# Score units of two banks that may take a third, P V sums in the last PSUM bank, a ring of exponentials, and two GELUs by tanh

## The chip, the cores and the metric

The kernel runs on one core of a Trainium2 chip. The metric is the device time of one execution in microseconds (us). Five engines work at the same time, each through its own queue in order: TensorE (PE, matrix products; PEld is its weight load), ScalarE (ACT, functions such as exp), VectorE (DVE, elementwise work and reductions), GpSimd (POOL), and SyncE (SP), which here only issues transfers. PSUM, where TensorE writes its results, has eight banks of 128 partitions x 512 float32 values; this text calls them b0 to b7.

## The reference

There are two layers, each an attention block and a mixer with an MLP, on 2048 tokens of 448 features with 16 heads of 28:

```python
x = x + _A_ref(_layernorm(x), A_wqkv, A_wo)
x = x + _B_ref(_layernorm(x), B_w1, B_w2, B_w3, B_w4)
x = x + _A_ref(_layernorm(x), A_wqkv, A_wo)
x = x + _B_ref(_layernorm(x), B_w1, B_w2, B_w3, B_w4)

def _A_ref(x, wqkv, wo):              # attention, 16 heads
    q, k, v = split(x @ wqkv)
    p = softmax(q @ k.T * Dh ** -0.5)
    return (p @ v) @ wo

def _B_ref(x, w1, w2, w3, w4):        # mixer, then MLP
    h = gelu(layernorm(x) @ w1)       # gelu in its tanh form
    g0, g1, g2, g3 = the four quarters of h's features, shifted by -1, +1, -2, +2 tokens
    x1 = x + concat(g0, g1, g2, g3) @ w2
    return x1 + gelu(layernorm(x1) @ w3) @ w4
```

## The kernel before

**The stream of score blocks.** A block is one head's scores for 512 (query, key) columns on 128 partitions: one PSUM bank. Both layers together have 2048 blocks, and their order is fixed: `segs` lists segments (a chunk of queries, a group of four heads, a range of key tiles) and `stream` their blocks. `t_scores` cuts the stream into units. An even unit has three blocks, in b0, b1, b2; an odd unit has two, in b3, b4 (`unit_banks`). One exponential of ScalarE (`t_exp`, L1892) reads a whole unit from PSUM and writes it, in bf16, to slots of the buffer `PT`, which has 15 slots. A unit's slots are fixed by its number: three pairs of units, five slots each. So unit u may write when P V has read unit u - 6. The scores of unit u + 2 go into the banks of unit u, and TensorE may start them when the exponential of unit u has ended.

**Blocks that VectorE takes.** Some blocks aren't given to ScalarE. `t_scores` takes a block further ahead in the stream and lets VectorE work out its exponential in five instructions (`d_first`, `d_chain`: L1736, L1763, L1765, L1767, L1770). Its scores stand either in the third bank of an even unit (rates `R_RATE`) or in a free shared bank (rates `D_RATE`). The tables of rates give, by stretch of the stream, the greatest share taken in this way.

**P V.** `t_pv` multiplies the exponentials by the values, eight blocks at a time, and sums a segment in one bank, b5, which it holds for the whole run. `t_norm` copies the sums out with VectorE (L1973, L1975).

**Shared banks.** All else that TensorE does goes through the list `MISC`: the projections of queries, keys and values, the output projection, the mixer's and the MLP's products (`mm4`, L1059: four column groups of 32 at a time). While the exponentials run, `misc` may take one of the first three names of the list. One of these is b5, which is never free, so there are two such banks, b6 and b7.

**The mixer and its GELU.** `t_mixA` works out the mixer's first product for a chunk of tokens. VectorE copies it out of PSUM (L2128), and its GELU is then done in one of two ways. Where `PAIR` names the chunk, one ScalarE instruction does all four feature groups (L2140), right after the GELU of an MLP group of tokens that `PAIR` names, so that both use one load of the function table (`ACT_TABLE_LOAD`). Otherwise `tanh_gelu` makes it from a tanh, which has the exponentials' table: a square (L2156, on GpSimd or VectorE), a VectorE instruction (L2157), the tanh (L2158), a VectorE instruction (L2159), for each feature group. `t_mixB` and `t_w4` go on with the MLP.

**Order.** `Sched` is a list scheduler that runs when the kernel is built: it has a cost for each operation, and ranks (`RANK`), rates, leads and first positions that say what goes first. Its result is an order of instructions on each engine's queue. Two further steps change that order: `P.rearranged(MOVES, WEAVE)` moves single operations, 370 of them, each named by its number, to written-out places, and `FILL_MORE` repeats six groups of filler matmuls. A filler (`filler`, L2385) is a product of the identity with itself into a bank that nobody uses, put in where TensorE has nothing to do in the plan (`keep_pe_busy`).

The last exponential is followed by the tail: `t_exp` sends the event `tail`, and the remaining MLP work then has all banks and plain GELUs on ScalarE (L2313, L2123).

Of the kernel before, what the change touches and what calls it, by code (L numbers as in the profile page):

```python
# [18 lines left out]
MOVES = (  # L19
# [147 lines left out]
    "stttsttttsttttstttsttsttsttsttttttttttvtttvttvtsttvstttvvtgttgvtvttgtgtvtvtgtvttsvtgtttdtttgttttttgttttvtttvtt",  # L167
    "tttttvtttttvtdtvttvttttttttttsttttsttttsttttsttttsttttsttttsttttsttttsttttsttttsttttsttttsttttsttttttttttttttv",
    "ttttdttttttttttvttttdttttttttttvttttdvttttdttttttttttvttttdttttttttttvttdvdd",
)  # L170

FILL_MORE = (
    (2714, 4), (2725, 9), (3749, 15), (5548, 4), (5564, 4), (9810, 14),
# [603 lines left out]
RHI = 7  # L777
# [1719 lines left out]
```

## Time and profile before

| what | value |
|---|---|
| median of 3 runs | 1024.59 us (1024.34 to 1025.14) |
| span of the profiled execution | 1022.4 us; its time outside the span isn't listed |
| ScalarE busy | 981.4 us (96%) |
| TensorE busy | 973.8 us (95%), of it fillers 150.1 us |
| VectorE busy | 811.0 us (79%) |
| first exponential starts, last one ends | 15.2 us, 968.4 us |
| exponentials | 782 instructions: 375 of three banks, 406 of two, one of one |
| blocks that VectorE takes | 109 |

A table of groups gives for each kind of instruction its count, the sum and the mean of the durations, and the engine's idle time ahead of it with what ended it. ScalarE starts its next instruction before the one ahead has left the pipeline, so the durations of neighbours overlap and their sum exceeds the busy time. The profile's times count from the first instruction.

### The profile page before, as it was taken

The page shows a single profiled execution, that of the slowest core. Times are in us where ns is not written, and L with a number is a line of the kernel's source. Part 1 is how long each engine was busy: PE and PEld are TensorE (multiplying, and loading weights), DVE is VectorE, ACT ScalarE, POOL GpSimd, SP SyncE. Part 2 cuts the span into 40 slices and gives each one's busy share as a digit, 9 for nine tenths or more (in the row PEclk, how much of TensorE's full clock was granted, in tenths as well). Part 3 has the DMA queues.
Part 4 walks back from the last instruction along what each step waited for, and adds up shares of the span by engine and source line. Part 5 has one row for each costly group of instructions (what it writes and reads, how often), then busy time and mean ns, then how long its engine had stood idle before and what let it go on. Part 6 is the DMA issues. An engine that isn't in the chain of part 4 may idle for free.

```text
span 1022.4 us, 36170 instructions
## 1 busy us (share of the span) xinstructions
PE 973.8 (95%) x16283; PEld 412.9 (40%) x16285; DVE 811.0 (79%) x1572; ACT 981.4 (96%) x894; POOL 292.3 (29%) x462
## 2 busy tenths in 40 slices
PE   8999999999999999999999999999999999999998
PEld 4332443443433254333433443433433433454565
DVE  8777999989888958876877868688898589866651
ACT  8999999999999999999999999999999999999942
POOL 3312021531453016252325112012624120532230
PEclk9999999999999999999999999999999999999999
DMA  4643413320321013131131024423302020121101
GB/s 126 161 111 117 119 45 79 53 39 23 76 61 28 13 37 96 23 48 34 48 111 38 33 69 134 141 66 99 65 25 37 17 68 16 31 57 31 26 12 33
DMA packets 99394, 62.57 MB, mean 61 GB/s; under 512 B 68712, under 2 KB 88552, under 8 KB 99240
## 3 DMA queue, kind: packets, MB, share of 16 engines
q1 hardware_dynamic: 99240, 60.27, 23.6%
q8 instruction: 127, 2.08, 0.9%
q14 instruction: 27, 0.22, 0.1%
HBM read 28.16 MB, written 16.76 MB: 44 GB/s over the span
## 4 chain that ended last, share of the span: by engine, by line
ACT 71%; PE 23%; DVE 4%; DMA 1%; issue 1%; DVEq 0%
ACT PT L1892 65%; PE ps L1059 14%; PE ps L1654 5%; PE ps L1050 4%; ACT h2T L2339 2%; ACT fb L2158 1%; PE ps L2385 1%; ACT L1892 1%; DVE PD L1770 0%; ACT hT L2140 0%; DVE h2T L2317 0%; DMA xT<-xn 0%; ACT L2339 0%; DMA obf<-in_A_x_dram 0%; DVE yd L1736 0%
## 5 line engine op out<-in xcount | busy, mean ns | idle before, releaser
L1892 ACT ACTIVATE PT<-ps 128x1024 bf16<-128x1024 f32 (+1 forms) x782 | 887.3, 1333 | 2.9 <-PE ps L1654 2.1
L1654 PE MATMUL ps<-qT,kT 32*128 32x512 bf16 (+1 forms) x2304 | 269.8, 335 | 24.2 <-ACT PT L1892 18.4
L1050 PE MATMUL ps<-PT,vaug 128*32 128x512 bf16 (+1 forms) x2420 | 246.1, 341 | 0.7 <-ACT PT L1892 0.2
L1059 PE MATMUL ps<-xT,w 128*32 128x512 bf16 (+4 forms) x2656 | 177.9, 344 | 4.2 <-DVE h2T L2317 2.2
L1654 PEld LDWEIGHTS ps<-qT,kT 32*128 32x128 bf16 x2304 | 69.7, 91 | 256.0 <-ACT PT L1892 227.0
L2385 PE MATMUL ps<-ident 128*32 128x256 bf16 x3524 | 150.1, 276 | 1.8 <-POOL ident L1144 1.5
L2385 PEld LDWEIGHTS ps<-ident 128*32 128x32 bf16 x3524 | 98.9, 97 | 28.5 <-issue 11.9
L1050 PEld LDWEIGHTS ps<-PT,vaug 128*32 128x32 bf16 x2420 | 74.0, 95 | 89.4 <-issue 71.0
L1999 POOL TENSOR_TENSOR otn<-ub,fb 128x512 bf16<-128x512 f32 (+1 forms) x31 | 34.7, 1120 | 210.3 <-DMA fb<-rscr 202.9
L1736 DVE TENSOR_SCALAR yd<-ps 128x512 int32<-128x512 f32 x109 | 74.6, 685 | 22.8 <-PE ps L1654 21.7
L1059 PEld LDWEIGHTS ps<-xT,w 128*32 128x32 bf16 (+1 forms) x2656 | 69.2, 95 | 56.7 <-issue 25.0
L1763 DVE SCALAR_TENSOR_TENSOR fb<-yd 128x512 f32<-128x512 uint16 x109 | 78.5, 724 | 0.8
L1765 DVE SCALAR_TENSOR_TENSOR fb<-fb,yd 128x512 f32<-128x512 f32 x109 | 77.9, 717 | 0.7
L1770 DVE SCALAR_TENSOR_TENSOR PD<-yd,PD 128x512 int16<-128x512 int16 x109 | 75.9, 698 | 1.6
L1059 PE MATMUL ps<-w,h2T 128*32 128x448 bf16 x1120 | 75.4, 355 | 1.1 <-ACT h2T L2339 1.0
L2317 DVE CAST h2T<-ps 128x512 bf16<-128x512 f32 (+1 forms) x70 | 44.4, 635 | 16.2 <-PE ps L1059 15.0
L1392 POOL TENSOR_TENSOR sq<-qT 128x512 bf16<-128x512 bf16 x24 | 28.5, 1190 | 96.2 <-DVE qT L1451 93.4
L1392 POOL TENSOR_TENSOR sq<-kT 128x512 bf16<-128x512 bf16 (+2 forms) x32 | 30.4, 950 | 83.0 <-DVE kT L1406 79.9
L1767 DVE TENSOR_SCALAR PD<-fb 128x512 bf16<-128x512 f32 x109 | 49.6, 456 | 1.0
L1059 PE MATMUL ps<-xT,wk_pad 128*32 128x512 bf16 (+2 forms) x576 | 47.6, 359 | 0.7 <-DVE kT L1406 0.3
L1654 PE MATMUL ps<-wk_pad,kT 32*128 32x512 bf16 x256 | 39.6, 384 | 4.6 <-ACT PT L1892 4.0
L1059 PE MATMUL ps<-xT,wq_pad 128*32 128x512 bf16 x512 | 43.2, 382 | 0.5 <-issue 0.5
(189 smaller groups left out, 1195.9 us busy)
## 6 DMA issues: line engine op xcount, KB each, us to landing
uscr<-ub SPq DMA_DIRECT2D x28, 256.0 KB
ub<-uscr SPq DMA_DIRECT2D x28, 256.0 KB, 6.8
fb<-rscr SPq DMA_DIRECT2D x24, 256.0 KB
xnd<-xn SPq DMA_DIRECT2D x28, 128.0 KB, 2.3
xd<-x_res SPq DMA_DIRECT2D x16, 224.0 KB, 2.1
x_res<-xd SPq DMA_DIRECT2D x16, 224.0 KB, 4.2
w<-in_B_w_dram SPq DMA_DIRECT2D x5, 448.0 KB, 6.0
obf<-in_A_x_dram SPq DMA_DIRECT2D x16, 112.0 KB
```

Of the source, the lines that this page charges most:

```text
L1050: return lambda e: e.matmul(out=out, lhsT=lhsT, rhs=rhs, start=start, stop=stop, **kw)
L1059: r.append(e.matmul(out=out[c:c + w, :], lhsT=lhsT[:, c:c + w], rhs=rhs, start=start, stop=stop, tile_position=(0, c)))
L1392: return both("sq", 0.15 + NW * 0.0018, 0.07 + NW * 0.00104, lambda e: e.tensor_tensor(out=sq[:, si, 0:NW], in0=src, in1=src, op=ALU.mult) ...
L1654: yield op("pe", (0.005 + NW * 0.00042) / nc_, lambda e, i=i, kc=kc, j=j, g=g, qt=qt, a=a, NW=NW, bank=bank: e.matmul(out=ps[:, bank, i * ...
L1736: yield op("dve", c_ps(512), lambda e: e.tensor_scalar(out=y, in0=ps[:, bi(bank), :], scalar1=SCALE * L2E * FS, scalar2=-126.0 * FS, op0=A ...
L1763: yield op(D_[0][0], D_[0][1], lambda e: e.scalar_tensor_tensor(out=q, in0=lo, scalar=E2 / E3 * FS, in1=lo, op0=ALU.add, op1=ALU.mult), re ...
L1765: yield op(D_[1][0], D_[1][1], lambda e: e.scalar_tensor_tensor(out=q, in0=q, scalar=E1 / E3 * FS * FS, in1=lo, op0=ALU.add, op1=ALU.mult) ...
L1767: yield op(D_[2][0], D_[2][1], lambda e: e.tensor_scalar(out=pdt, in0=q, scalar1=E3 / FS ** 3, scalar2=E0, op0=ALU.mult, op1=ALU.add), rea ...
L1770: yield op(D_[3][0], D_[3][1], lambda e: e.scalar_tensor_tensor(out=pdt.bitcast(I16), in0=hi, scalar=128.0, in1=pdt.bitcast(I16), op0=ALU. ...
L1892: yield op("act", 0.069 + n * w * 0.000833, lambda e, bk=bk, s0=s0, n=n, w=w: e.activation(out=PT[:, s0:s0 + n, 0:w], in_=ps[:, bk[0]:bk[0 ...
L2317: ev = op("dve", c_ps(m * NW), lambda e, hr=hr, pv=pv: e.tensor_copy(out=hr, in_=pv), reads=[("ps", bi(b))], writes=hk, touch=[b])
L2385: return [e.matmul(out=ps[32 * c:32 * c + 32, bi(b), 0:256].rearrange("p (a n) -> p a n", n=128), lhsT=ident[:, 32 * c:32 * c + 32], rhs=i ...
```

## The change

- `unit_banks`: an odd unit may have three banks: b3, b4 and b5. Before it forms an odd unit, `t_scores` adds a credit from the table `BX` (1 per odd unit where the table has no entry). With a full credit it asks for b5. It doesn't ask if b6 is in use or if an operation waits for a list that has b5 in it (`BXF`). If b5 is given, the unit takes three blocks, and the exponential gives b5 back.
- P V sums in b7 instead of b5, and holds it. The shared banks while exponentials run are therefore b6 and b5.
- A unit's slots in `PT` are no longer fixed: units follow each other in a ring of 15 slots, which starts again at slot 0 where a unit doesn't fit before the end. The exponential waits for P V of the blocks that had these slots last.
- `PAIR` loses (1, 4) and (1, 8): the GELUs of the mixer for tokens' tiles 4 to 7 and 8 to 11 of layer two are done by tanh.
- `MOVES`, `WEAVE` and `FILL_MORE` are empty: the order is the scheduler's own, and no filler group is repeated.
- The scheduler's numbers (`RANK`, `R_RATE`, `D_RATE`, `Q_LEAD`, first positions of K, Q and V, of weights, doubts and the windows for fillers) are others. The shares of `R_RATE`, weighted by blocks, sum to 187 blocks instead of 227, those of `D_RATE` to 276 instead of 284; `BX` asks on average for 0.80 of the odd units.

```diff
-MOVES = (
...
-WEAVE = (
...
-FILL_MORE = (
-    (2714, 4), (2725, 9), (3749, 15), (5548, 4), (5564, 4), (9810, 14),
-)
+MOVES = ()
+WEAVE = ()
+
+FILL_MORE = ()
...
-RHI = 7
+RHI = 9
...
-DTH = 0.4
-XSHUT = (8, 83)
+DTH = 0.396
+XSHUT = (12, 79)
...
-DDTH = 1.3
+DDTH = 1.876
...
-Sched.TARGET = 0.695
+Sched.TARGET = 0.684
...
+BX = {47: 0.25, 39: 0.75, 36: 0.25, 41: 0.5, 34: 0, 32: 0, 5: 1, 2: 0, 25: 0, 20: 0.75, 42: 0, 33: 1, 50: 0.25, 59: 0.25, 58: 0.75, 22: 0, 12: 0, 31: 1, 9: 1, 4: 1}
+BXD = 1.0
+BXF = 1
...
-PAIR = {(0, 12): 7, (1, 4): 0, (1, 8): 3}
+PAIR = {(0, 12): 7}
...
-        MISC = ["b6", "b7", "b5", "b4", "b3", "b2", "b1", "b0"]
+        MISC = ["b6", "b5", "b7", "b4", "b3", "b2", "b1", "b0"]
...
-            return (0, 1, 2)[:len(units[u])] if u % 2 == 0 else (3, 4)[:len(units[u])]
+            return (0, 1, 2)[:len(units[u])] if u % 2 == 0 else (3, 4, 5)[:len(units[u])]
...
                 lim = 3 - u % 2
+                if u % 2 == 1 and pos < len(stream):
+                    wide_t[0] += BX.get(seg_b0[stream[pos][0]] // 32, BXD)
+                    if wide_t[0] >= 1.0:
+                        got = None
+                        if not (BXF and (SC.busy.get("b6", False) or any(t_[3][0] == "acq" and "b5" in t_[3][1] for t_ in SC.pendq))):
+                            got = yield ("try", [["b5"]])
+                        if got is not None:
+                            lim = 3
+                            extra_bank.add(u)
+                            wide_t[0] -= 1.0
+                        wide_t[0] = min(wide_t[0], 1.0)
+                base = ring_at[0] if ring_at[0] + lim <= 15 else 0
                 while pos < len(stream) and len(un) < lim:
-                    if len(un) == 2 and rb is None and SC.load("dve", DWIN) < DTH:
+                    if len(un) == 2 and rb is None and u % 2 == 0 and SC.load("dve", DWIN) < DTH:
...
-                    home[blk] = ("pt", 5 * ((u // 2) % 3) + 3 * (u % 2) + len(un))
+                    home[blk] = ("pt", base + len(un))
...
                 units.append(un)
+                ring_at[0] = base + len(un)
+                before[u] = [owner[s_] for s_ in range(base, base + len(un)) if s_ in owner]
+                for k_, b_ in enumerate(un):
+                    owner[base + k_] = b_[0:2]
...
-                if u >= 6:
-                    for (si, kb, j) in units[u - 6]:
-                        yield ("wait", ("pv", si, kb))
+                for (si, kb) in before[u]:
+                    yield ("wait", ("pv", si, kb))
...
+                if u in extra_bank:
+                    yield ("rel", "b5")
...
-            yield ("acq", ["b5"])
+            yield ("acq", ["b7"])
...
-                                yield op("pe", max(0.018, 0.0015 + NW * 0.0001042), mm(ps[32 * j:32 * j + 32, 5, 0:NW], vaug[:, vs, 32 * (4 * g + j):32 * (4 * g + j) + 32],
+                                yield op("pe", max(0.018, 0.0015 + NW * 0.0001042), mm(ps[32 * j:32 * j + 32, 7, 0:NW], vaug[:, vs, 32 * (4 * g + j):32 * (4 * g + j) + 32],
...
-        SC.fill = (0.12, filler, ["b6", "b7", "b0", "b1", "b2", "b3", "b4"], lambda b: ("ps", bi(b)), [("ident",)])
+        SC.fill = (0.12, filler, ["b6", "b5", "b0", "b1", "b2", "b3", "b4"], lambda b: ("ps", bi(b)), [("ident",)])
```

More of the change, by code (lines that the diff above doesn't have):

```diff
@@ L802 @@
 SMALL = [11, 12]
-W_POS = (6, 9, 17, 5, 5, 5, 25, 21)
-V_FIRST = 1.366
-K_FIRST = (0.756, 0.932, 1.363)
-Q_FIRST = (0.531, 1.956, 2.405)
+BX = {47: 0.25, 39: 0.75, 36: 0.25, 41: 0.5, 34: 0, 32: 0, 5: 1, 2: 0, 25: 0, 20: 0.75, 42: 0, 33: 1, 50: 0.25, 59: 0.25, 58: 0.75, 22: 0, 12: 0, 31: 1, 9: 1, 4: 1}
+BXD = 1.0
+BXF = 1
+W_POS = (5, 7, 17, 8, 3, 7, 28, 23)
+V_FIRST = 1.113
+K_FIRST = (0.484, 0.789, 1.051)
+Q_FIRST = (0.3, 1.564, 2.358)
 Q_EARLY = 1
@@ L814 @@
 COLD = 6.0
-Sched.DOUBT2 = {"dma": 1.5, "pool": 0.2, "dve": 0.5, "act": 0.5, "pe": 0.0}
+Sched.DOUBT2 = {'dma': 1.5, 'pool': 0.2, 'dve': 0.5, 'act': 0.5, 'pe': 0}
 Sched.EARLY = 0.1
-Sched.DOUBT = {"dma": 0.8, "pool": 0.6, "dve": 0.05, "act": 0.05}
+Sched.DOUBT = {'dma': 0.8, 'pool': 0.6, 'dve': 0.05, 'act': 0.05}
+Sched.LCRED = 0.3
 def PENORM(L, ch, g):
@@ L903, in build_kernel @@
     units = []
+    extra_bank = set()
+    owner = {}
+    before = {}
+    ring_at = [0]
+    wide_t = [0.0]
     home = {}
@@ L1851, in t_scores @@
                 units.append(un)
+                ring_at[0] = base + len(un)
+                before[u] = [owner[s_] for s_ in range(base, base + len(un)) if s_ in owner]
+                for k_, b_ in enumerate(un):
+                    owner[base + k_] = b_[0:2]
+                if u in extra_bank and len(un) < 3:
+                    extra_bank.discard(u)
+                    yield ("rel", "b5")
                 blks, banks = list(un), [b_ for b_ in unit_banks(u)]
@@ L1892, in t_exp @@
                 yield op("act", 0.069 + n * w * 0.000833, lambda e, bk=bk, s0=s0, n=n, w=w: e.activation(out=PT[:, s0:s0 + n, 0:w], in_=ps[:, bk[0]:bk[0] + n, 0:w], func=ACT.Exp, scale=SCALE),
-                         reads=[("ps", b) for b in bk], writes=[("pt", s0 + k) for k in range(n)], tab="exp")
+                         reads=[("ps", b) for b in bk], writes=[("pt", s0 + k) for k in range(n)], tab="exp", touch=["b5"] if u in extra_bank else [])
                 for b in bk:
                     yield ("dead", "b%d" % b)
+                if u in extra_bank:
+                    yield ("rel", "b5")
                 yield ("sig", ("ex", u))
@@ L1920, in t_pv @@
                             yield ("wait", ("v", L, kt))
-                    yield ("ready", [home[(si, kb, j)] for kb in batch for j in range(4)] + ([("psw", 5)] if done == 0 else []))
+                    yield ("ready", [home[(si, kb, j)] for kb in batch for j in range(4)] + ([("psw", 7)] if done == 0 else []))
                     for kb in batch:
@@ L1972, in t_norm @@
             if first:
-                yield op("dve", c_ps(NW), lambda e: e.tensor_copy(out=u, in_=ps[:, 5, 0:NW]), reads=[("ps", 5)], writes=[uk])
+                yield op("dve", c_ps(NW), lambda e: e.tensor_copy(out=u, in_=ps[:, 7, 0:NW]), reads=[("ps", 7)], writes=[uk])
             else:
-                yield op("dve", c_ps2(NW), lambda e: e.scalar_tensor_tensor(out=u, in0=u, scalar=fct[:, L, PI[L, p], g:g + 1], in1=ps[:, 5, 0:NW],
+                yield op("dve", c_ps2(NW), lambda e: e.scalar_tensor_tensor(out=u, in0=u, scalar=fct[:, L, PI[L, p], g:g + 1], in1=ps[:, 7, 0:NW],
                                                                             op0=ALU.mult, op1=ALU.add),
-                         reads=[("ps", 5), uk, ("fct", L, PI[L, p])], writes=[uk])
+                         reads=[("ps", 7), uk, ("fct", L, PI[L, p])], writes=[uk])
             yield ("sig", ("ucopied", si))
```

124 lines of the change are left out of this document (10 added, 114 removed), and 46 rows, old and new, of the table MOVES.

## The prediction

> **What bounds the kernel now.** I read the page's head and its chain of waits first, then ScalarE's groups, its waits, and the stretches in which the bound changes.
>
> ```profile
> span 1022.4 us, 36170 instructions
> PE 973.8 (95%) x16283; PEld 412.9 (40%) x16285; DVE 811.0 (79%) x1572; ACT 981.4 (96%) x894; POOL 292.3 (29%) x462
> ACT 71%; PE 23%; DVE 4%; DMA 1%; issue 1%; DVEq 0%
> ```
>
> The chain that ended last is 71% ScalarE and 23% TensorE. Stretches (columns: TensorE, weight loads, VectorE, ScalarE, GpSimd busy, granted clock, DMA) say where each rules:
>
> ```profile
> 15.20:968.40 953.20, 910.02 (x14875) 373.30 (x14879) 780.12 (x1482) 949.30 (x846) 278.82 (x424) 1.00 0.25 61
> 892.60:903.20 10.60, 9.99 (x312) 7.85 (x306) 4.99 (x12) 10.56 (x5) 0.73 (x1) 1.00 0.05 16
> 903.20:968.40 65.20, 64.27 (x1160) 29.84 (x1156) 47.81 (x99) 65.18 (x63) 18.86 (x33) 1.00 0.17 42
> 968.40:1019.40 51.00, 51.00 (x1178) 32.42 (x1168) 18.63 (x38) 20.12 (x33) 8.19 (x20) 1.00 0.06 19
> ...
> 892.60:903.20 10.60, 6.86 (x244) 6.17 (x236) 1.00 0.05 16
> 903.20:968.40 65.20, 0.00 (x0) 0.00 (x0) 1.00 0.17 42
> ```
>
> The last two rows are of the fillers (L2385) alone. From the first exponential to the last (953.2 us) ScalarE idles 953.20 - 949.30 = 3.9 us: this phase is ScalarE's sum. The tail, 1022.4 - 968.4 = 54 us, is TensorE's: busy for all of 51 us. TensorE is full from 903.2 on, with no filler; just before, from 892.6 to 903.2, fillers take 6.86 us of it. So work that TensorE could do before 903 comes off the tail.
>
> **1. Fewer exponentials.** What does an instruction cost beside its data?
>
> ```profile
> L1892 ACT ACTIVATE PT<-ps 128x1536 bf16<-128x1536 f32 x375 | 582.8, 1554 | 2.2 <-PE ps L1654 1.5
> L1892 ACT ACTIVATE PT<-ps 128x1024 bf16<-128x1024 f32 x406 | 453.4, 1130 | 0.7 <-PE ps L1654 0.6
> ...
> L1892 ACT ACTIVATE PT<-ps 128x512 bf16<-128x512 f32 x1 | 0.6, 598 | 0.0
> L1892 ACT ACTIVATE PT<-ps 128x1536 bf16<-128x1536 f32 x39 | 62.8, 1611 | 0.0
> L1892 ACT ACTIVATE PT<-ps 128x1024 bf16<-128x1024 f32 x40 | 47.6, 1190 | 0.0
> 111.45 89.31 ACT L1892 ACTIVATE PT<-ps 128x1024 bf16<-128x1024 f32 x79
> ```
>
> The first three rows are the whole run. A bank more costs 1554 - 1130 = 424 ns. That would leave 1130 - 848 = 282 ns for an instruction, but neighbours overlap. The last three rows are one unbroken stretch: 79 instructions, 39 x 3 + 40 x 2 = 197 banks, in 89.31 us. 197 x 0.424 = 83.5, so an instruction costs (89.31 - 83.5) / 79 = 0.073 us, not 0.28.
>
> ScalarE's blocks: 375 x 3 + 406 x 2 + 1 = 1938. 782 are 391 pairs of units with 1938 / 391 = 4.96 blocks, 2.96 in the even unit and 2 in the odd. If no odd unit gets b5, 782 stay: 0 us. If all do, 1938 / 5.96 x 2 = 650: 132 fewer, 132 x 0.073 = -9.6 us. How often is b5 free? It is one of two shared banks now, and it is asked for only while b6 is free too:
>
> ```profile
> 511.00:562.00 51.00, 33.49 (x478) 12.23 (x471) 1.00 0.27 74
> L2317 DVE CAST h2T<-ps 128x512 bf16<-128x512 f32 x42 | 28.9, 689 | 10.0 <-PE ps L1059 9.1
> ```
>
> The stretch is of L1059 alone. A busy one keeps a bank for 33.5 us of products, and about 478 / 16 = 30 evacuations at 0.69 = 20.6 us: 54 of 102 bank-us, without the waits between. Both banks are then free for (1 - 0.53)^2 = 0.22 of the time at most; in quieter stretches more often. With a credit for 0.80 of the odd units I take 0.35: 1938 / 5.31 x 2 = 730 units, 52 fewer, **-3.8 us**.
>
> **2. TensorE's side of a unit.**
>
> ```profile
> 301.31 0.10 PEld L1654 LDWEIGHTS ps<-qT,kT 32*128 32x128 bf16 x3 [0.37 <-ACT PT L1892]
> 301.31 0.39 PE L1654 MATMUL ps<-qT,kT 32*128 32x512 bf16 x3
> ...
> 302.34 0.39 PE L1654 MATMUL ps<-qT,kT 32*128 32x512 bf16 x2
> PEld ps L1654 <- ACT PT L1892: 258.8, 668, 2.0
> ```
>
> Two or three blocks take the same 0.39 us, and ahead of them TensorE stands 0.37 us for a bank (258.8 us over 668 waits). A unit less frees up to 0.76 us of TensorE. Before 903 that becomes filler: 0. From 903 to 968 ScalarE runs 63 instructions; at most 9 units fewer would give 6.8 us, at 0.35 some 4, 3 us. But ScalarE is full there as well, so the end of the exponentials doesn't move by it, only the backlog of the tail. I count this under 4.
>
> **3. Two GELUs by tanh, on ScalarE and VectorE.**
>
> ```profile
> L2140 ACT ACTIVATE hT<-hT 112x2048 bf16<-112x2048 bf16 x2 | 3.8, 1906 | 0.0
> L2158 ACT ACTIVATE fb<-fb 112x512 f32<-112x512 f32 x16 | 12.2, 788 | 0.7 <-DVE fb L2157 0.7
> 414.86 1.04 ACT fb L2158 x2
> L2157 DVE SCALAR_TENSOR_TENSOR fb<-fb,hT 112x512 f32<-112x512 f32 x16 | 14.0, 882 | 0.6 <-POOL fb L2156 0.6
> L2159 DVE SCALAR_TENSOR_TENSOR hT<-fb,hT 112x512 bf16<-112x512 f32 x16 | 11.2, 702 | 2.4 <-ACT fb L2158 2.3
> ```
>
> Two GELUs of 1.906 = 3.8 us go, eight tanhs come: by the chain's pair 0.52 each, 4.2; at 0.788 alone, 6.3. So +0.4 (to +2.5); I take **+0.4**, the row where they stand in a full queue. The table loads stay: both GELUs used the load of an MLP group, which remains.
>
> ```profile
> L1763 DVE SCALAR_TENSOR_TENSOR fb<-yd 128x512 f32<-128x512 uint16 x109 | 78.5, 724 | 0.8
> L1765 DVE SCALAR_TENSOR_TENSOR fb<-fb,yd 128x512 f32<-128x512 f32 x109 | 77.9, 717 | 0.7
> L1770 DVE SCALAR_TENSOR_TENSOR PD<-yd,PD 128x512 int16<-128x512 int16 x109 | 75.9, 698 | 1.6
> L1736 DVE TENSOR_SCALAR yd<-ps 128x512 int32<-128x512 f32 x109 | 74.6, 685 | 22.8 <-PE ps L1654 21.7
> L1767 DVE TENSOR_SCALAR PD<-fb 128x512 bf16<-128x512 f32 x109 | 49.6, 456 | 1.0
> ```
>
> VectorE gets 8 x (0.882 + 0.702) = 12.7 us and perhaps squares, out of 953.2 - 780.1 = 173 us of idle time: 0. If they displaced blocks instead: a block costs VectorE the five rows, 3.28 us, and saves ScalarE 0.424, so four blocks go back, +1.7. The new rates and gates could move the 109 blocks by some 8 either way, 3.4 us. I take 0: the sums of the tables fall, while VectorE's gate (`DDTH`) opens.
>
> **4. The tail.**
>
> ```profile
> 891.82 0.68 DVE L2128 TENSOR_SCALAR hT<-ps 112x512 bf16<-112x512 f32 x1
> 892.59 1.28 ACT L2339 ACT_TABLE_LOAD   x1
> 893.09 6.62 PE L2385 MATMUL ps<-ident 128*32 128x256 bf16 x236
> 893.89 6.18 ACT L2339 ACTIVATE h2T<-h2T 128x7168 bf16<-128x7168 bf16 x1
> 899.97 1.90 ACT L2140 ACTIVATE hT<-hT 112x2048 bf16<-112x2048 bf16 x1
> 902.01 0.94 PE L1059 MATMUL ps<-w,hT 112*32 112x448 bf16 x16 [0.20 <-ACT hT L2140]
> ```
>
> This is the mixer's GELU for tiles 8 to 11, which becomes tanh. Its input is ready at 892.5, its output at 901.9; meanwhile TensorE makes 6.62 us of fillers, and the next real product waits for that output. With tanhs ahead of the table load the products could fill that hole. At most 6.9 us leave a stretch that is TensorE's to the end, with point 2 at most 10.7. Nothing leaves if the scheduler puts the tanhs after the table load, or if the last tokens' own chain sets the end. I take **-5**.
>
> **5. The order.** `MOVES` and `FILL_MORE` go. No row shows ScalarE under the plain order. Lower end 0: the shorter queue may need no repair. Upper end: from the end of an exponential TensorE needs 0.37 + 0.39 us and a hand-over, of the 0.92 us that a two-bank exponential lasts (2 x 0.424 + 0.073). Had one unit in ten (73) one product of four column groups in the way (0.2 us), that were 15 us. The nearest row is today's 3.9 us of idle time; I take as much again, **+4**.
>
> At no cost: the bank of P V (the same instructions); the ring (ScalarE's waits list none for P V, and 15 slots stay, two of which a lap may skip; up to +2); `misc`'s list in the tail. No DMA is added.
>
> **Sum.** -3.8 + 0.4 - 5 + 4 = -4.4. The profiled execution spans 1022.4, and 2.2 us lie between that and the median, 1024.6, if it ran like the three timed ones. 1022.4 - 4.4 + 2.2 = **1020.2 us**, faster by 0.43%. A measurement of this kernel tells some 0.2% (2 us) from no change.
>
> **Rivals.**
> - *The plain order loses more than the units give.* For it: the written-out order holds ScalarE's idle time at 3.9 us in 953, and the margin above is 0.1 to 0.2 us for each unit. Against: a three-bank odd unit leaves 0.42 us more margin. It decides from 8.4 + 2 = 10.5 us on; at 15 the time is 1024.6 - 8.4 + 15 = 1031. Slower.
> - *The shared bank starves the projections.* With b5 lent for about 2 us in a third of the odd units (137 x 2 = 274 bank-us of 1906), products come late, and the tail gets longer by a group's backlog. One MLP group of 14 products is about 14 x (0.23 + 0.69) = 13 us of one bank: 1020.2 + 9 = 1029 where two thirds of it stay on the path.
> - *It rarely does what it says.* b5 free for one odd unit in ten: -1 instead of -3.8, and -3 in the tail: 1025.
> - *All of it at once.* All odd units wide (-9.6), the whole hole filled (-6.9), the order free: 1024.6 - 9.6 - 6.9 + 0.4 = 1008.5.
> - *The clock falls.* The granted clock is 1.00 in every stretch above, the fillers' hole included. With fewer fillers, a stretch as long as that hole at half clock would cost its length, some 7 us, where TensorE is the bound: 1027.
>
> The Trainium skill, "TensorE: Matmul & The Clock Gate", Part 1: The HAM clock gate, says that an array idle for more than about 3.4 us falls to half its clock until it has been busy for a window. By that rule the six repeated filler groups matter only where TensorE would stand longer than that; the trace agrees as far as it goes, with a clock of 1.00 throughout, and can't show the fall.
>
> **Chances.** My forecast 0.34 (1016 to 1022.5), with the larger gain 0.14; the order 0.27, starved projections 0.12, the clock 0.04; rarely done 0.09. Faster 0.48, same 0.09, slower 0.43. About 0.1 lies below 1010 and 0.1 above 1032, where the order and the projections come together. The forecast's own range is 1015 to 1023.
>
> **What will show it.** Right: some 730 exponentials, over 400 of them of 1536 columns; ScalarE's idle time between exponentials under 9 us; 24 tanhs of 112x512; no fillers in the last GELU visit and a tail under 50 us. Wrong: ScalarE's waits for L1654 over 15 us (order), the tail over 58 us (projections), a granted clock under 1.00, or under 100 blocks on VectorE.

## The result, and the profile after

| | before | changed |
|---|---|---|
| time, median | 1024.46 us | 1035.68 us (1035.05 to 1038.23) |
| profiled execution: span | 1022.4 us | 1036.5 us |
| first exponential starts | 15.2 us | 16.0 us |
| first to last exponential: length | 953.1 us | 966.3 us |
| ... ScalarE busy in it | 949.3 us | 952.5 us |
| ... ScalarE idle in it | 3.9 us | 13.8 us |
| tail behind the last exponential | 54.1 us | 54.2 us |
| exponentials (blocks in them) | 782 (1938) | 771 (1943) |

The change makes the kernel slower: ratio 1.0115 [1.0101, 1.0130]. The forecast was 1020.2 us (1015 to 1023), with some 0.1 of the chances below 1010 and 0.1 above 1032. The 14.1 us between the two spans are 0.8 ahead of the first exponential, 3.3 of work on ScalarE, 9.9 of idle time between exponentials and 0.1 in the tail. The profiled execution of the changed kernel is the slowest of its four (1038.2 us, the others 1035.1 to 1036.3), so these parts add up to more than the 11.2 us between the medians.

The head of the changed kernel's page and its chain of waits:

```profile
span 1036.5 us, 34822 instructions
PE 961.9 (93%) x15627; PEld 402.5 (39%) x15629; DVE 822.9 (79%) x1575; ACT 984.6 (95%) x888; POOL 295.0 (28%) x459
...
ACT 63%; PE 28%; DVE 6%; DMA 2%; issue 1%; POOL 0%; SPq 0%; DVEq 0%; ACTq 0%
```

ScalarE's share of the chain falls from 71% to 63%, and TensorE and VectorE take it. TensorE is busy for 12 us less in a span that is 14 us longer: it stands idle for 74.6 us instead of 48.6.

Its exponentials and tanhs, in groups by shape:

```profile
L1767 ACT ACTIVATE PT<-ps 128x1536 bf16<-128x1536 f32 x401 | 602.2, 1535 | 12.6 <-PE ps L1511 9.2 <-PE ps L907 2.4
L1767 ACT ACTIVATE PT<-ps 128x1024 bf16<-128x1024 f32 x370 | 404.8, 1106 | 0.9 <-PE ps L1511 0.8
...
L2035 ACT ACTIVATE fb<-fb 112x512 f32<-112x512 f32 x24 | 16.2, 701 | 0.0
```

401 x 3 + 370 x 2 = 1943 blocks. Exponentials alternate between even and odd units; counted along the trace, 371 of the 401 wide ones are even and 30 odd. So b5 was lent to 30 of 385 odd units. ScalarE waits 10.0 us for scores (L1511) and 2.4 us for P V (L907), where before it waited 2.1 us for scores (1.5 + 0.6) and not for P V.

Stretches of 5 us of the changed kernel (columns as in the prediction, the granted clock third from the end):

```profile
430.00:435.00 5.00, 4.24 (x73) 1.66 (x71) 4.93 (x10) 5.00 (x5) 0.00 (x0) 1.00 0.02 5
435.00:440.00 5.00, 4.57 (x58) 2.24 (x55) 2.88 (x5) 4.50 (x5) 2.76 (x3) 0.66 0.08 26
...
760.00:765.00 5.00, 3.58 (x39) 1.08 (x36) 4.25 (x8) 5.00 (x7) 0.00 (x0) 1.00 0.00 0
765.00:770.00 5.00, 3.86 (x34) 1.04 (x38) 3.43 (x7) 4.77 (x6) 0.00 (x0) 0.75 0.02 3
770.00:775.00 5.00, 5.00 (x45) 1.30 (x41) 2.64 (x5) 3.02 (x3) 0.78 (x2) 0.50 0.16 56
775.00:780.00 5.00, 5.00 (x59) 1.34 (x55) 3.02 (x8) 3.45 (x4) 2.67 (x5) 0.73 0.13 26
845.00:850.00 5.00, 3.61 (x72) 1.69 (x68) 5.00 (x7) 5.00 (x5) 3.04 (x3) 1.00 0.17 34
850.00:855.00 5.00, 3.85 (x48) 1.28 (x51) 4.91 (x9) 3.88 (x4) 0.00 (x0) 0.78 0.01 3
855.00:860.00 5.00, 5.00 (x58) 1.37 (x55) 2.08 (x3) 3.43 (x3) 0.00 (x0) 0.88 0.00 0
```

The clock falls three times, and in the six stretches of low clock ScalarE is idle for 7.0 of 30 us (5 less 4.50, 4.77, 3.02, 3.45, 3.88 and 3.43). A stretch in which TensorE was busy for 3.6 to 4.2 us of 5 stands ahead of each fall, and no single wait of TensorE there lasts over 1.2 us. Cut at the falls themselves, the stretch ahead of each and the fall are:

```profile
433.00:436.40 3.40, 2.27 (x42) 0.86 (x41) 2.65 (x5) 3.40 (x4) 1.33 (x2) 0.99 0.10 33
436.40:439.80 3.40, 3.40 (x41) 1.77 (x37) 2.18 (x4) 3.10 (x4) 1.44 (x2) 0.50 0.02 7
764.10:767.50 3.40, 1.84 (x19) 0.53 (x17) 2.88 (x5) 3.40 (x4) 0.00 (x0) 0.99 0.01 2
767.50:777.70 10.20, 10.20 (x79) 2.43 (x79) 5.72 (x13) 6.84 (x6) 2.74 (x6) 0.50 0.15 41
849.40:852.80 3.40, 1.74 (x30) 0.66 (x30) 3.37 (x7) 2.78 (x3) 0.00 (x0) 1.00 0.00 0
852.80:856.20 3.40, 3.40 (x32) 0.82 (x24) 2.84 (x5) 1.70 (x2) 0.00 (x0) 0.50 0.02 5
```

Each fall is to half the clock, and the three last 3.4, 10.2 and 3.4 us. In the 3.4 us ahead of them TensorE was busy for 2.3, 1.8 and 1.7 us. The prediction had not seen a clock under 1.00 anywhere before.

### The profile page after: what moved, and what is told of

It is laid out like the page before. It is cut to its first block, busy times and chain, and to the rows that moved or that the text cites. A ratio compares the mean times of both kernels' runs of the same rounds, so it can differ in the third digit from the quotient of the medians.

```text
span 1036.5 us, 34822 instructions
## 1 busy us (share of the span) xinstructions
PE 961.9 (93%) x15627; PEld 402.5 (39%) x15629; DVE 822.9 (79%) x1575; ACT 984.6 (95%) x888; POOL 295.0 (28%) x459
## 4 chain that ended last, share of the span: by engine, by line
ACT 63%; PE 28%; DVE 6%; DMA 2%; issue 1%; POOL 0%; SPq 0%; DVEq 0%; ACTq 0%
ACT PT L1767 58%; PE ps L916 16%; PE ps L1511 6%; PE ps L907 5%; ACT h2T L2216 2%; ACT fb L2035 1%; DVE fb L1622 1%; DVE yd L1593 1%; DMA xT<-xnd 1%; ACT L1767 0%; ACT L2216 0%; PE ps L2262 0%; DVE fb L1620 0%; DMA xT<-xn 0%; DVE PD L1627 0%
## 5 line engine op out<-in xcount | busy, mean ns | idle before, releaser
L1511 PE MATMUL ps<-qT,kT 32*128 32x512 bf16 (+1 forms) x2304 | 265.3, 335 | 35.8 <-ACT PT L1767 30.1
L907 PE MATMUL ps<-PT,vaug 128*32 128x512 bf16 (+1 forms) x2425 | 248.3, 344 | 1.0 <-DVE ub L1852 0.6
L916 PE MATMUL ps<-xT,w 128*32 128x512 bf16 (+3 forms) x2816 | 187.6, 341 | 7.0 <-DVE h2T L2194 2.8
L1511 PEld LDWEIGHTS ps<-qT,kT 32*128 32x128 bf16 x2304 | 68.8, 91 | 267.9 <-ACT PT L1767 243.0
L2262 PE MATMUL ps<-ident 128*32 128x256 bf16 x2868 | 129.0, 278 | 4.8 <-DVE yd L1593 2.9
L907 PEld LDWEIGHTS ps<-PT,vaug 128*32 128x32 bf16 x2425 | 73.8, 95 | 94.2 <-issue 76.3
L916 PEld LDWEIGHTS ps<-xT,w 128*32 128x32 bf16 (+1 forms) x2816 | 76.4, 95 | 60.7 <-issue 24.8
L2262 PEld LDWEIGHTS ps<-ident 128*32 128x32 bf16 x2868 | 84.7, 98 | 27.2 <-issue 7.7
L1593 DVE TENSOR_SCALAR yd<-ps 128x512 int32<-128x512 f32 x103 | 70.5, 686 | 17.8 <-PE ps L1511 16.9
L916 PE MATMUL ps<-w,h2T 128*32 128x448 bf16 x1120 | 73.5, 354 | 1.6 <-DVE x_res L2232 1.0
L1622 DVE SCALAR_TENSOR_TENSOR fb<-fb,yd 128x512 f32<-128x512 f32 x103 | 73.7, 717 | 1.0
L1627 DVE SCALAR_TENSOR_TENSOR PD<-yd,PD 128x512 int16<-128x512 int16 x103 | 72.4, 705 | 1.3
L1624 DVE TENSOR_SCALAR PD<-fb 128x512 bf16<-128x512 f32 x104 | 46.4, 447 | 1.3
L1511 PE MATMUL ps<-wk_pad,kT 32*128 32x512 bf16 x256 | 39.6, 400 | 7.3 <-ACT PT L1767 6.5
L916 PE MATMUL ps<-xT,wq_pad 128*32 128x512 bf16 x512 | 44.0, 382 | 1.6 <-DMA xT<-xnd 1.0
L916 PE MATMUL ps<-w,hT 112*32 112x448 bf16 x512 | 40.4, 375 | 1.1 <-DVE yd L1593 0.8
```

Source lines behind the costliest of these rows:

```text
L907: return lambda e: e.matmul(out=out, lhsT=lhsT, rhs=rhs, start=start, stop=stop, **kw)
L916: r.append(e.matmul(out=out[c:c + w, :], lhsT=lhsT[:, c:c + w], rhs=rhs, start=start, stop=stop, tile_position=(0, c)))
L1511: yield op("pe", (0.005 + NW * 0.00042) / nc_, lambda e, i=i, kc=kc, j=j, g=g, qt=qt, a=a, NW=NW, bank=bank: e.matmul(out=ps[:, bank, i * ...
L1593: yield op("dve", c_ps(512), lambda e: e.tensor_scalar(out=y, in0=ps[:, bi(bank), :], scalar1=SCALE * L2E * FS, scalar2=-126.0 * FS, op0=A ...
L1622: yield op(D_[1][0], D_[1][1], lambda e: e.scalar_tensor_tensor(out=q, in0=q, scalar=E1 / E3 * FS * FS, in1=lo, op0=ALU.add, op1=ALU.mult) ...
L1624: yield op(D_[2][0], D_[2][1], lambda e: e.tensor_scalar(out=pdt, in0=q, scalar1=E3 / FS ** 3, scalar2=E0, op0=ALU.mult, op1=ALU.add), rea ...
```

## The experiments

All medians stand against the kernel before on the same chip, 1023.7 to 1024.4 us. "Idle" is ScalarE's idle time from the first to the last exponential, and a clock is the granted clock; both are of the one profiled execution.

### e1 and e4: the written-out order and its fillers

```diff
 # e1, on the kernel before          # e4, on the kernel before
-MOVES = (...)                        -FILL_MORE = ((2714, 4), ...)
-WEAVE = (...)                        +FILL_MORE = ()
-FILL_MORE = (...)
+MOVES = WEAVE = FILL_MORE = ()
```

> The kernel before with the written-out order taken away: MOVES, WEAVE and FILL_MORE are empty, all else is as before. Theory A (the loss of the change is the loss of the written-out order): 1035 us, 1030 to 1040; ScalarE idles 10 to 18 us between the first and the last exponential where before idles 3.9 us, and the tail after the last exponential stays at 54 us within 1. Theory B (the shared bank, the ring and the narrower projections cost, the order little): 1024.5 to 1028 us, idle time under 7 us.

> The kernel before with FILL_MORE empty alone: six filler groups are issued once instead of 4, 9, 15, 4, 4 and 14 times, the written-out order stays. Theory A with the clock as a part of it (fewer fillers let TensorE's clock fall): 1026 to 1034 us, with two to five windows of 10 us in which the granted clock is under 0.95, and 2 to 9 us more idle time of ScalarE there. Rival (the fillers' repeats matter to nothing): 1024.5 within 1 us, granted clock 1.00 in every window.

e1: 1028.14 us, 1.0033 [1.0019, 1.0047]; idle 6.2 us. e4: 1024.03 us, 1.0000 [0.9990, 1.0010]; the clock is 1.00 throughout. Theory A missed in both. e1 comes out at theory B's upper end, and e4 is as its rival said. Taking the lists away costs 3.9 us and not the 11 of the change; the repeats of fillers are worth nothing in the median where the written-out order stands.

The mean clock of an execution is known for every run, and it differs between executions of one kernel. Of e1's ten, the five at 1.000 took 1025.5 to 1028.3 us and the five at 0.997 or 0.998 took 1028.1 to 1030.3. Four of e4's ten stand at 0.998 (1024.1, 1024.1, 1025.8 and 1026.9 us). So one profile shows the falls of one execution.

### e2, e3 and e6: the lent bank, with two sets of numbers

```diff
 # e2: changed kernel, numbers and PAIR of before; e6: the same, and
 # e3: changed kernel with its own numbers, and
-BX = {47: 0.25, 39: 0.75, ...}
-BXD = 1.0
+BX = {}
+BXD = 0.0
```

> The changed kernel with the numbers of before put back (rates, gates, ranks, first positions, windows for fillers, PAIR), so without the two GELUs by tanh: left of the change are the third bank for odd units, P V in the last bank, the ring of 15 slots and the empty lists. To be read against the kernel before without its lists. Theory A: within 5 us of that kernel, so 1030 to 1040, since the structure itself is nearly free and brings nearly nothing: under 60 odd units with three banks. Theory B: 6 to 15 us slower than that kernel, with ScalarE waiting for scores or the tail longer by that much.

> The changed kernel with no odd unit of three banks (BX empty, BXD 0): b5 is then a shared bank only; ring, P V bank, tanhs and numbers stay. Theory A: 1036 to 1043 us, because 30 exponentials of 1536 columns become 30 of 1024 and some 15 instructions more at 0.07 us are 1 us, and the order is a plain one as well. Theory B (lending b5 to units is what costs): 1024 to 1030 us, with idle time of ScalarE between exponentials back under 7 us.

> The changed kernel with the numbers of before and no odd unit of three banks: of the change only the ring of slots, the bank of P V and the empty lists are left. To be read against the kernel before without its lists (1028.1 us) and the same kernel with some 30 odd units of three banks (1040.9 us). Theory D (the ring and the bank cost nothing, the odd units of three banks cost 12 us with these numbers): 1027 to 1030 us. Theory E (the ring costs): 1034 to 1041 us, with ScalarE waiting for products of P V.

e6: 1028.43 us, 1.0041 [1.0029, 1.0053], idle 4.4 us: the ring, and P V in b7, cost nothing against e1 (theory D). e2: 1040.87 us, 1.0157 [1.0135, 1.0179], idle 16.1 us: with the numbers of before, the kernel with 32 odd units of three banks is 12.4 us slower. e3: 1037.35 us, 1.0128 [1.0107, 1.0148], idle 14.1 us: with the numbers of the change, taking them away gains nothing; the 1.7 us that it loses lie within the two intervals. So theory B holds with the numbers of before and theory A with those of the change. Where does e3, which lends no bank, lose its time? TensorE and ScalarE around its largest wait, in order of time:

```profile
779.86 0.39 PE L1511 MATMUL ps<-wk_pad,kT 32*128 32x512 bf16 x2
780.18 1.27 PE L2262 MATMUL ps<-ident 128*32 128x256 bf16 x40
781.28 4.31 PE L916 MATMUL ps<-xT,w 128*32 128x384 bf16 x92
785.42 0.39 PE L907 MATMUL ps<-PT,vaug 128*32 128x512 bf16 x4
...
785.84 1.45 ACT L1767 ACTIVATE PT<-ps 128x1536 bf16<-128x1536 f32 x1 [6.04 <-PE ps L907]
```

ScalarE needs slots of the ring, and so products of P V (L907). In TensorE's queue ten groups of fillers and then 92 matmuls of projections stand ahead of them, the latter 4.3 us with their waits for VectorE to empty a bank. That is 6.0 of the 14.1 us of idle time. It is an order of one queue and has nothing to do with a lent bank.

### e10: the bank lent, but not used

```diff
 # on the changed kernel with the numbers and PAIR of before
-                            lim = 3
                             extra_bank.add(u)
...
-                if u in extra_bank and len(un) < 3:
+                if u in extra_bank and len(un) < 2:
```

> The changed kernel with the numbers of before, in which an odd unit asks for b5 and holds it until its exponential is done as in the change, but takes two blocks all the same. Read against the same kernel without asking (1028.4 us) and with three blocks in the lent bank (1040.9 us). Theory F (the lent bank is missing to the projections, which then come late for scores): 1033 to 1042 us, with fewer product matmuls done by the 900th block than the 2604 of the kernel without asking. Theory G (the three blocks themselves cost: P V's slots come free later, the stream of scores runs ahead of the projections): 1027 to 1031 us.

1038.49 us, 1.0139 [1.0121, 1.0156]; idle 12.4 us, and a tail of 58.5 us instead of 54.2. The kernel that only lends is 10 us slower than e6, as theory F has it; but its sign failed: 2664 products were done by the 900th block, more than the 2604 of e6 (2544 in e2). The largest wait is again one of order:

```profile
438.38 2.37 ACT L1766 ACTIVATE PT<-ps 128x1024 bf16<-128x1024 f32 x2 [5.22 <-PE ps L907]
```

TensorE makes some 4 us of products of V and K in a row ahead of that P V. Whether the bank or only the new order costs the 10 us, this pair doesn't tell.

### e13 to e16: is it the bank or the order?

```diff
 # e13 (no bank lent) and e14 (lent): one number of before changed
-Q_LEAD = {(0, 0): 0, (0, 1): 4, (0, 2): 45, (0, 3): 11, ...
+Q_LEAD = {(0, 0): 0, (0, 1): 4, (0, 2): 45, (0, 3): 13, ...
 # e15 (no bank lent) and e16 (lent): RANK and Q_LEAD of the change
```

> The kernel of the ring, the bank of P V and the empty lists alone (numbers of before, no odd unit of three banks, 1028.4 us), with one number changed: Q_LEAD of layer one's last chunk 13 instead of 11. No bank is lent and no unit is wider. Theory F (lending b5 costs): 1026 to 1031 us, as without the change of the number. Theory H (any new order of the same work lands on other stalls, and the 1028 of this set of numbers is a good draw): 1032 to 1042 us, with a stall of ScalarE of 2 us or more behind products in TensorE's queue, or low clock.

> The same number changed in the kernel with some 32 odd units of three banks (1040.9 us before the number's change). Theory F: 1036 us or more, and 8 us or more above its narrow twin. Theory H: 1030 to 1042 us, above or below its narrow twin, within 5 us of it.

> The kernel of the ring, the bank of P V and the empty lists alone, with the ranks (RANK) and Q's leads (Q_LEAD) of the changed kernel, all other numbers of before, no odd unit of three banks. Theory F: 1026 to 1031 us. Theory H: 1030 to 1040 us.

> The same ranks and leads with some 33 odd units of three banks. Theory F: 8 us or more above its narrow twin. Theory H: within 5 us of its narrow twin, on either side.

| numbers | no bank lent | lent to 30 to 33 units | difference |
|---|---|---|---|
| of before | 1028.43 (e6) | 1040.87 (e2) | +12.4 |
| of before, one lead 13 for 11 | 1044.14 (e13) | 1046.86 (e14) | +2.7 |
| of before, RANK and Q_LEAD of the change | 1035.90 (e15) | 1049.22 (e16) | +13.3 |
| of the change | 1037.35 (e3) | 1035.68 (changed) | -1.7 |

The left column is nearly the same work in four orders (e3 has the two tanhs, and each has its own few more or fewer blocks on VectorE), and it spans 15.7 us; one lead changed by two is worth all of that. It is theory H's mechanism, though e13 and e14 lie above the ranges that H gave. The kernel that lends is 6.7 us slower on the mean of the four pairs, but the differences of 2.7 and -1.7 lie within the intervals of their runs. Both theories hold in part, then, and four pairs don't size the bank's share: two pairs go with F by 12 and 13 us, two with H. The losses sit in other places each time. In e13 in ScalarE's idle time, in e15 in the tail:

```profile
15.83:987.30 971.47, 917.02 (x14880) 373.80 (x14882) 785.45 (x1487) 950.70 (x847) 282.31 (x424) 0.99 0.24 60
```

```profile
15.76:971.56 955.80, 903.54 (x14562) 366.55 (x14561) 780.73 (x1476) 949.56 (x845) 269.23 (x413) 1.00 0.24 61
971.56:1033.80 62.24, 58.11 (x1344) 37.03 (x1344) 22.82 (x47) 21.46 (x36) 11.50 (x25) 1.00 0.08 23
```

e13 idles 971.47 - 950.70 = 20.8 us; e15 only 6.2, but has a tail of 62.2 us.

### e5 and e9: the clock

```diff
+FILL_AT = {4622: [('z', 4)], 4636: [('z', 1)], 4650: [('z', 3)], 8011: [('z', 4)], ...}
+        def zeros(e):   # columns of ident against others of its columns: adds 0 to the bank of P V
+            return [e.matmul(out=ps[32 * c:32 * c + 32, 7, 0:256]..., lhsT=ident[:, 32 * c:32 * c + 32],
+                             rhs=ident[:, 64 - 64 * (c // 2):128 - 64 * (c // 2)]..., start=False, stop=False, ...) for c in range(4)]
+        P = P.filled(FILL_AT, make)   # the same order, these operations put in
```

> The changed kernel, its order kept, with 38 groups of four matmuls more on TensorE at nine places: ahead of scores at which TensorE stood idle for 0.2 to 1.2 us in the 5 to 10 us before the three stretches of low clock (around 430 to 436, 757 to 768 and 848 to 853 us). They add zeros to the bank of P V, or fill it while it is free, and wait for no shared bank. Theory C (about half of the 13.8 us of ScalarE's idle time is TensorE's clock at 0.5 to 0.8 in these stretches): granted clock 1.00 there, idle time between exponentials 6 to 9 us, 1029 to 1032 us, so 4 to 7 us faster than the changed kernel. Rival (the waits come from the order and lower the clock, not the other way round): the clock falls as before or the waits stay, 1034.5 to 1038 us.

> The changed kernel, its order kept, with 188 groups of four matmuls at 51 places: the nine of the first such kernel and 42 more, wherever TensorE stood idle for 0.3 us or more while sums of P V were under way. If what is left of the low clock costs as well (two stretches of 5 us at 0.66 in the first such kernel): no stretch of 5 us under 0.95 up to 960 us, ScalarE idle for 6 to 8 us between exponentials, 1030 to 1032 us. If the added matmuls stand in the way of scores as much as the clock gives: 1032.5 to 1035 us. If the clock was all of the loss: 1027 or less.

e5: 1032.89 us, 1.0087 [1.0073, 1.0102], idle 9.3 us; the three falls are gone, and two of 3.4 us each stand elsewhere (105 to 110 us at 0.67, 450 to 455 at 0.66). That is just past theory C's ranges (9 us idle, 1032 us). e9: 1030.63 us, 1.0066 [1.0052, 1.0080], idle 7.3 us, no stretch under 0.95. Its stretches around the second fall, and the whole phase:

```profile
765.00:770.00 5.00, 4.92 (x78) 1.92 (x78) 3.87 (x8) 5.00 (x5) 0.63 (x2) 1.00 0.03 5
770.00:775.00 5.00, 4.97 (x88) 2.03 (x76) 4.63 (x12) 5.00 (x6) 3.27 (x8) 1.00 0.28 82
...
16.09:974.84 958.75, 913.96 (x14973) 376.83 (x14972) 791.83 (x1484) 951.48 (x840) 277.83 (x419) 1.00 0.25 61
```

With the same order and 752 matmuls more on TensorE, the kernel is 5.0 us faster than the changed one, and ScalarE idles 6.5 us less. All of the ranges that I had set for the case that the low clock costs hold. So the clock made nearly half of the loss: waits of the order leave TensorE idle, the clock falls, scores take 0.61 us instead of 0.39, and ScalarE waits again.

### e17: one wait repaired by hand

```diff
+EARLIER = ((1884, 1840),) + tuple((a, 1875) for a in (1896, 1897, 1898, 1900, 1901, 1902, 1903, 1905))
```

> The kernel with 188 groups of zeros more (1030.6 us), in which nine operations are issued earlier: at 183 us VectorE reads the finished sum of P V out of its bank ahead of three rows of layer norm instead of behind them, and the first eight products of the next sum stand ahead of fillers. ScalarE waits 1.58 us at 186.6 there for slots of the ring. If the ring's wait is an order in two queues and no lack of slots: that wait is under 0.3 us, ScalarE's idle time 5.5 to 6 us, 1028.5 to 1030 us. If the slots are lacking: the wait stays, 1030 to 1031.5 us.

1032.28 us, 1.0082 [1.0067, 1.0098], idle 7.7 us: no gain over e9, perhaps a loss. ScalarE, VectorE and TensorE, in order of time:

```profile
189.02 3.95 ACT L1792 ACTIVATE PT<-ps 128x1536 bf16<-128x1536 f32 x3 [0.15 <-PE ps L1536]
...
191.97 0.51 DVE L1141 TENSOR_SCALAR xn<-x_res,mv,mst 128x448 bf16<-128x448 f32 x1 [1.60 <-POOL mst L1980]
192.40 0.68 DVE L1618 TENSOR_SCALAR yd<-ps 128x512 int32<-128x512 f32 x1
...
193.14 0.51 PE L2287 MATMUL ps<-ident 128*32 128x256 bf16 x12 [1.35 <-DVE yd L1618]
193.58 0.39 PE L1536 MATMUL ps<-qT,kT 32*128 32x512 bf16 x2
...
194.01 2.44 ACT L1792 ACTIVATE PT<-ps 128x1024 bf16<-128x1024 f32 x2 [1.04 <-PE ps L1536]
```

The wait for the ring, 1.58 us at 186.6, is gone (0.15 is left), so slots weren't lacking. Some 4 us later a new one takes 1.04 us back: VectorE stands 1.60 us at a layer norm for GpSimd, the read of a bank (`yd`) is queued behind it, a filler on TensorE waits 1.35 us for that bank, and the scores are queued behind the filler. None of the kernels that do the whole work beats the kernel before, and e9 is the best of those with the change's own numbers.

### e7: what an instruction costs

```diff
-lambda e: e.activation(out=PT[:, s0:s0 + n, 0:w], in_=ps[:, bk[0]:bk[0] + n, 0:w], ...)
+lambda e: [e.activation(out=PT[:, s0 + a:s0 + z, 0:w], in_=ps[:, bk[0] + a:bk[0] + z, 0:w], ...)
+           for (a, z) in ([(0, 2), (2, 3)] if n == 3 else [(0, n)])]
```

> The kernel before, its written-out order kept, in which each exponential of 1536 columns is two instructions, one of 1024 and one of 512: 375 instructions more with the same data. If an instruction costs ScalarE 0.073 us beside its data, as worked out from one unbroken stretch: 375 x 0.073 = 27 us slower, 1047 to 1056 us. If it costs 0.28 us, as the mean durations of the two widths give: 105 us slower, about 1130 us. If it costs nothing: 1024 to 1028 us.

1042.50 us, 1.0176 [1.0162, 1.0191]: 18.3 / 375 = 0.049 us an instruction. ScalarE between the first and the last exponential of the split kernel:

```profile
15.21:987.18 971.97, 916.31 (x14876) 373.72 (x14879) 780.88 (x1482) 969.69 (x1220) 276.59 (x424) 1.00 0.24 60
```

Busy for 20.4 us more than before, 0.054 each; 1.6 us come back as idle time falls to 2.3 us. The mean durations (0.28) are far off, and my 0.073 was a third to a half too high, as far as an instruction added within a unit tells of a unit's own. The Trainium skill, "ScalarE: Activation LUTs", What ACT_TABLE_LOAD costs, gives 0.186 us beside the data for an activation with immediate scale and bias, of which neighbours overlap some 0.093; by an estimate from it 0.093 us would be left. The run shows half of that.

### e8 and e11: the tail

```diff
 # e8, on the changed kernel
-PAIR = {(0, 12): 7}
+PAIR = {(0, 12): 7, (1, 4): 0, (1, 8): 3}
 # e11, on the kernel before: every second inner product behind 969 us, 24 of them
+        thin = [i for i in range(len(P.all)) if P.all[i].t_end > THIN_T and hasattr(P.args[i][1], "thin")][0:2 * THIN_N:2]
```

> The changed kernel with the two GELUs of layer two's mixer back on the GELU table (PAIR as before), all else as changed; eight tanhs and 16 products of VectorE go, two GELUs of 112x2048 come, and the scheduler orders the rest anew. If the tanhs cost only their own time (8 of about 0.5 us against 3.8 us): 1033 to 1038 us and a tail longer by up to 5 us where products wait for that GELU. If the tanhs are what loses the time: 1024 to 1030 us.

> The kernel before, its written-out order kept, in which 24 products of the tail (each four matmuls of 448 or 512 columns, placed some 3 to 19 us behind the last exponential) are one matmul of 32x8: part of MLP sums is left out. It says whether the tail is TensorE's sum, as term 4 of the prediction took it. If so: 24 x 0.2 = 4.8 us less, 1019 to 1021 us. If the tail is a chain of the last tokens' own operations: 1023 to 1024.5 us.

e8: 1036.32 us, 1.0120 [1.0103, 1.0136], idle 9.6 us. The stretch behind the last exponential, of e8, and then of the kernel before and of e11:

```profile
976.96:1035.20 58.24, 55.01 (x1270) 34.72 (x1263) 19.45 (x40) 20.66 (x35) 8.84 (x20) 0.99 0.09 21
```

```profile
968.34:1022.40 54.06, 51.11 (x1182) 32.48 (x1170) 19.41 (x39) 20.16 (x33) 8.19 (x20) 1.00 0.07 22
967.85:1019.70 51.85, 48.45 (x1110) 32.12 (x1098) 19.26 (x39) 20.11 (x33) 8.17 (x20) 1.00 0.07 23
```

Without the tanhs the tail is 4.1 us longer than the changed kernel's 54.2, and ScalarE's idle time 4.2 shorter; as the order is another one too, neither figure is the tanhs' alone. The time is the same. e11: 1022.26 us, 0.9980 [0.9971, 0.9989], and a tail 2.2 us shorter (51.9 for 54.1). TensorE's busy time in it falls by 51.1 - 48.5 = 2.7 us and not by the 4.8 that I had expected, as the 24 single matmuls are still busy for 4.1 us in all. So four fifths of what e11 took from TensorE left the time, which goes with a tail that is TensorE's sum.

### e12: the bank for units alone

```diff
-        MISC = ["b6", "b5", "b7", "b4", "b3", "b2", "b1", "b0"]
+        MISC = ["b6", "b7", "b4", "b3", "b2", "b1", "b0", "b5"]
 # BX = {}, BXF = 0
```

> The changed kernel with b5 kept for units: it stands last in the list of shared banks and units ask for it at every odd unit, even if b6 is in use. Some 190 odd units of three banks instead of 30, and projections, fillers and VectorE's blocks have one bank. If the rival of starved projections holds: over 1080 us, ScalarE idle for over 40 us between exponentials, most of it before scores. If one bank does for the projections: 1025 to 1040 us.

1142.53 us, 1.1149 [1.1122, 1.1177]. 191 odd units of three banks, 732 exponentials, and 101 us of idle time. Only 19 us of it are waits for scores, of which I had expected most; the large ones are for VectorE, 27.4 us at one GELU (hT) and 21.3 us at two operations on `fct`. That is half of the odd units, where the prediction counted on 0.35, and the projections can't have the bank at all. So it isn't the price of lending as often as the prediction counted on, and shows only which way that price goes.

## Why the prediction was wrong

**Step 1, fewer exponentials: -3.8 forecast, +3.0 measured** (ScalarE's busy time between the first and the last exponential, less what its other instructions add to it, went from 879.9 to 882.9 us). The 0.35 failed: b5 was lent to 0.08 of the odd units, about the share of the rival "it rarely does what it says". It was a choice above the working's own 0.22, which was an upper bound of a busy stretch. That both banks are free in a fifth of a stretch need not hold at the moment at which a unit asks, as fillers, VectorE's blocks and waits between products are also in the banks; which of them kept b5 or b6 taken isn't shown. 11 instructions fewer at 0.05 are -0.6 us. Five blocks more on ScalarE are 5 x 0.424 = +2.1: VectorE made 105 instead of 110, with the two and the one that went through another buffer and aren't in the prediction's 109. The prediction had taken 0 for them, within 3.4. Some 1.1 of the 1.5 us that are left go with the waits: in e9, with the same order and 6.5 us less of idle time, the exponentials take 881.8 us. The rest I can't place.

**Step 2, TensorE's side: nothing measured,** as nothing was counted beside step 4. One reading in it was wrong. The 258.8 us are idle time of the weight loads' queue; the matmuls themselves wait far less ahead of these scores in the whole kernel before:

```profile
L1654 PE MATMUL ps<-qT,kT 32*128 32x512 bf16 (+1 forms) x2304 | 269.8, 335 | 24.2 <-ACT PT L1892 18.4
```

So a unit less frees far less than 0.37 us of TensorE's time; by this profile TensorE works at something else during most of it.

**Step 3, the tanhs: +0.4 forecast, +0.2 measured.** 24 tanhs of 112x512 are there, the table loads between the first and the last exponential stay at twelve; all tanhs of the phase take 18.2 us instead of 14.2, GELUs of hT 3.7 less. Right.

**Step 4, the tail: -5 forecast, +0.1 measured.** The hole is filled, with 28 filler matmuls left of 244 in the last GELU visit. But no product left the tail. The products in it (L1059 before, L916 in the changed kernel and in e8) are, in this order:

```profile
968.34:1022.40 54.06, 48.62 (x1136) 29.92 (x1124) 1.00 0.07 22
982.33:1036.50 54.17, 48.62 (x1136) 32.53 (x1132) 1.00 0.09 27
976.96:1035.20 58.24, 51.81 (x1208) 31.93 (x1208) 0.99 0.09 21
```

1136 matmuls and 48.62 us stand behind the last exponential in both kernels. That the tail is TensorE's was right, and e11 bears it out. What failed is that the -5 was reckoned from today's tail: under the change's numbers, the kernel without the two tanhs (e8) leaves 1208 products to a tail of 58.2 us, and the changed kernel comes 4.1 us below that, back to 54.2. The step's own gain was near its forecast, then, as far as e8 can tell, and the new order had lost as much; the sum had no price for that, as step 5 priced the order by ScalarE's idle time alone. The step's bound of 10.7 doesn't follow either: 6.9 and the 3 of step 2 are 9.9.

**Step 5, the order: +4 (0 to 15) forecast, +9.9 of idle time measured.** For the order that was taken away e1 measured 3.9 us, but that the forecast met it is luck: it was a guess (as much again as today's idle time), and in e1 the idle time rose by only 2.3 us. The failed sentence is "the nearest row is today's 3.9 us": rows of before speak of one order, and the change makes another one. Orders of nearly the same work lie 15.7 us apart. My upper end, 15 us, was the better guide than my value.

Which part of the change made this loss? The ring and P V's bank cost nothing (e6 against e1), the lent bank nothing under these numbers (e3), the two tanhs nothing (e8), the plain order 3.9 us (e1). What is left are the change's own numbers: from e6 to e3, which differ in them and in the tanhs, the time rises by 8.9 us, and `RANK` and `Q_LEAD` alone give 7.5 (e15).

**Of the rivals,** "the plain order loses more than the units give" came nearest, with "the clock falls" on top: 0.04 was far too little for what e9 sizes at 5 us. "The shared bank starves the projections" may hold in e12 and in two of the four pairs, but not in the changed kernel's own pair. Of the 14.1 us between the profiled executions, -0.6 + 2.1 + 9.9, with 0.8 at the start, are 12.2. The signs that I named went both ways: idle time over 9 us and a clock under 1.00 were said; waits for scores over 15 us, a tail over 58 us and fewer than 100 blocks on VectorE did not come. One sign of being right came by luck: 401 exponentials have 1536 columns, but 371 of them are even units and only 30 are lent ones.

**The rule on the clock.** In the changed kernel the clock fell where TensorE was busy for half to two thirds of the 3.4 us ahead, with no single wait over 1.2 us, and e9 held it up with a few groups of matmuls in gaps of 0.3 to 1.2 us. The Trainium skill, "TensorE: Matmul & The Clock Gate", Part 1: The HAM clock gate, speaks of an idle window of about 3.4 us, and I had argued from it that fillers matter only at such gaps. The same part also tells of a kernel in which short idle times between groups of matmuls were enough, which I had not used; the trace agrees with that. An idle gap of 3.4 us isn't needed, then. What share of idle time it takes is open: stretches of 5 us under 4.0 us busy stand at a clock of 1.00 too, 14 in the changed kernel and 4 in the kernel before.

What stays open is what the lent bank costs by itself. e3 finds no cost under these numbers, and the three other pairs 2.7 to 13.3 us. Nor does any run size, wait by wait, what the new order costs beside the clock.

## What to carry to other kernels

A planner that orders in-order queues by estimated times gives a new order for every number and every unit's size, and the orders differ by more than most changes do. Price a change that makes the planner order anew by the spread of its orders (here 16 us of 1028, by one lead changed by two), not by the waits of the one order that the profile shows; and measure the change under several sets of numbers before it is called good or bad. Look at the granted clock wherever TensorE stands idle for a part of the time: here its falls cost 5 of the 11 us, on top of the waits that brought them about.

## What the runs showed of the hardware

- TensorE's granted clock falls to one half for some 3.4 us or a multiple, without any idle gap of that length: ahead of the changed kernel's three falls TensorE was busy for 1.7 to 2.3 of 3.4 us.
- In stretches of 5 us up to 960 us of the profiled executions, the granted clock fell under 0.95 at least once in thirteen of the fifteen kernels of the scheduler's own order (not in e9 and e17, with the most added matmuls), and in none of the four with the written-out order. In e5 the falls moved to other places, and executions of one kernel differ.
- An activation more for the same data costs ScalarE 0.05 us in an unbroken row, where the listed durations suggest 0.28.
- A wait taken out of one in-order queue came back at two thirds of its size through three other queues (e17).
